# A new order for all steps of a delta-rule and MLP kernel, with forty instead of 26 filler products in its head

## The chip, the core and the metric

The kernel runs on one core of a Trainium2 chip. A core has five engines that run side by side, each through its own sequence of instructions: TensorE (PE, with its weight loads as PEld), VectorE (DVE), ScalarE (ACT), GpSimd (POOL) and SyncE (SP, which only issues transfers here). They wait for each other and for transfers on semaphores. The metric is the device time of one execution in microseconds (us); the median of several runs is compared.

## What is computed

The reference has two blocks. The first is a delta rule for 4 batches, 8 heads, 768 positions and head size 48: 32 independent states of 48 x 48, updated position by position.

```
k_n = k / (norm(k) + 1e-6)
for t in range(768):
    y[t]  = q[t] @ state
    v_old = state^T k_n[t]
    state = state + beta[t] * outer(k_n[t], v[t] - v_old)
```

Its output, laid side by side over the heads, is x with 768 positions of 384 features per batch. The second block is `x + relu(layernorm(x) * g @ w_ch1) @ w_ch2`, with w_ch1 of 384 x 1536 and w_ch2 of 1536 x 384. All numbers are 32-bit floats; the weights arrive as pairs of 32-bit words and are converted on the chip.

## The kernel before

**Chunks.** The 768 positions are cut into 12 chunks of 64. For each chunk TensorE forms the products of the keys with one another ("gram", L606 for chunks 0 to 4, L674 in a joint form later) and of keys with queries (L637, or jointly in L674). The triangular system of a chunk is inverted row by row on VectorE: for chunk 0 alone in a short form of 15 pairs of operations (L752 and L759, the near inverse), completed by two groups of small products on TensorE ("near products", L806: first xn x kt, then, after ScalarE's L809, xt x xn) and by a predicated copy on VectorE (L813); for two later chunks at once in 31 pairs (L843 and L850, the big inverse).

**The recurrence** runs chunk by chunk (`recur`): products with the state (L880), three solves (L902) with a copy on ScalarE (L908) or a subtraction on VectorE (L906) between them, the output y (L913), the state's update (L923), the layer normalization (L956 to L968) and the turned, scaled copy `xnt`. For chunk 0 there is no state yet, so it begins with the solves.

**The MLP** of a chunk follows its recurrence. For chunks 0 to 2 its first layer is done in plain products (L1178), for later chunks by fifteen block products with sums around them (L1094, with VectorE's L1107 and POOL's L1077). The second layer is plain for chunk 0 (L1200) and done by seven block products later (L1275, with POOL's L1261 and L1300). The weights are fetched in 12 pieces of 768 KB from ScalarE's queue and converted by ScalarE (L514, L522), VectorE (L519) and POOL (L532).

**The head.** Until the first MLP has its input, TensorE has little to do. Fillers are put there: 26 products of the identity with a broadcast column, 256 columns wide (`zeros`, L1358; each runs as two passes, so the profile counts 52), and three wider ones (`fill`, L544). They write half of a PSUM bank that nobody reads. The function `emit` lets other steps depend on them in no way (`or d.name == "warm"`), so they can stand anywhere in TensorE's sequence before that bank's half is wanted; nothing waits for them except what stands behind them on TensorE.

**The order.** The program first lists some 2,780 steps with what they read and write, without issuing anything. Then `line.emit(ORDER)` issues them in the order that the tuple `ORDER` names, by their numbers in the list. `in_this_order` ties each engine's instructions, and the transfers issued by SP and ScalarE, to that order. So `ORDER` sets the sequence of every engine and of both queues; between engines only data dependencies count. A transfer on these two queues also waits until the transfer eight places before it has landed, as eight semaphores are used in turn.

```
def emit(self, order):
    done = set()
    for n in order:
        s = self.steps[n]
        assert all(d.n in done or d.name == "warm" for d in s.deps), (n, s.key)
        done.add(n)
        s.fn()
```

Of the kernel before, what the change touches and what calls it, by code (L numbers as in the profile page):

```python
# [57 lines left out]
def pool(n):  # L58
# [5 lines left out]
WARM = 26  # L64
ORDER = (
    6, 7, 23, 5, 0, 59, 40, 60, 15, 8, 21, 4, 10, 20, 27, 16, 17, 219, 31, 26, 22, 69, 75, 29, 46, 35, 88, 89, 90, 67, 28, 25, 76, 92, 91, 93, 12, 94,
    1, 18, 2, 13, 126, 127, 19, 128, 129, 95, 3, 130, 30, 24, 131, 132, 133, 135, 9, 125, 134, 78, 65, 79, 61, 62, 81, 32, 385, 84, 34, 37, 42, 33,
    99, 101, 100, 50, 102, 41, 56, 86, 103, 104, 80, 47, 51, 48, 36, 64, 74, 38, 39, 82, 71, 96, 109, 107, 98, 66, 58, 97, 70, 110, 106, 108, 105, 53,
    322, 52, 44, 323, 202, 204, 190, 111, 114, 116, 115, 192, 117, 113, 72, 77, 87, 118, 119, 112, 121, 120, 179, 54, 68, 180, 43, 45, 321, 324, 169,
    136, 137, 138, 139, 140, 141, 142, 143, 144, 145, 146, 147, 148, 149, 150, 151, 152, 153, 154, 11, 155, 156, 170, 157, 158, 159, 160, 161, 162,  # L70
    203, 163, 164, 165, 171, 172, 166, 167, 191, 220, 205, 193, 173, 168, 174, 221, 175, 222, 122, 357, 181, 223, 14, 184, 352, 176, 196, 211, 177,
    206, 182, 124, 123, 194, 55, 224, 225, 226, 227, 228, 230, 231, 232, 233, 234, 235, 236, 237, 238, 239, 240, 241, 212, 242, 178, 243, 244, 245,
    246, 247, 229, 248, 249, 250, 251, 355, 252, 85, 293, 294, 295, 57, 296, 213, 326, 214, 215, 253, 183, 254, 255, 216, 256, 195, 257, 367, 297,
    188, 83, 561, 186, 258, 187, 259, 298, 299, 200, 301, 300, 260, 189, 382, 383, 63, 302, 303, 358, 304, 325, 319, 261, 198, 307, 305, 327, 262,
    306, 310, 263, 308, 328, 185, 197, 264, 311, 49, 265, 312, 73, 320, 266, 368, 360, 387, 388, 317, 267, 309, 703, 313, 390, 389, 268, 199, 269,
    329, 318, 343, 384, 315, 314, 316, 337, 567, 207, 333, 335, 330, 331, 270, 271, 272, 273, 570, 339, 340, 341, 342, 274, 275, 208, 276, 277, 359,
    391, 278, 392, 338, 566, 336, 279, 280, 427, 209, 332, 334, 425, 361, 426, 201, 394, 344, 372, 428, 429, 210, 362, 431, 353, 430, 432, 393, 217,
    218, 345, 435, 433, 281, 282, 283, 284, 285, 286, 287, 288, 289, 350, 351, 436, 290, 291, 292, 354, 386, 395, 439, 346, 434, 437, 370, 396, 705,
    568, 569, 563, 736, 560, 707, 564, 565, 841, 735, 369, 571, 348, 740, 716, 714, 701, 712, 840, 440, 349, 488, 438, 737, 739, 373, 715, 713, 397,
    711, 356, 717, 710, 441, 363, 442, 562, 398, 399, 464, 365, 445, 489, 400, 375, 487, 371, 465, 446, 490, 491, 449, 492, 493, 494, 495, 497, 496,  # L80
    498, 499, 500, 501, 502, 503, 374, 504, 364, 366, 401, 404, 405, 402, 406, 403, 407, 409, 410, 408, 411, 414, 376, 450, 451, 466, 467, 468, 469,
    718, 412, 479, 572, 452, 470, 471, 377, 443, 505, 453, 454, 506, 413, 507, 415, 416, 421, 508, 509, 510, 573, 417, 574, 444, 380, 472, 455, 456,
    423, 511, 512, 513, 514, 515, 378, 516, 517, 422, 518, 519, 447, 418, 379, 448, 480, 381, 419, 576, 733, 473, 474, 457, 520, 424, 475, 577, 420,
    575, 578, 521, 738, 743, 702, 522, 523, 747, 579, 998, 748, 704, 746, 745, 843, 997, 524, 525, 526, 527, 528, 529, 706, 485, 481, 996, 580, 742,
    749, 708, 709, 606, 476, 458, 459, 460, 461, 744, 750, 850, 581, 607, 848, 993, 582, 612, 851, 583, 613, 618, 608, 609, 530, 531, 532, 533, 584,
    482, 534, 719, 585, 610, 720, 619, 624, 614, 721, 625, 611, 616, 724, 615, 725, 620, 535, 536, 537, 639, 538, 539, 540, 541, 542, 483, 484, 543,
    544, 545, 546, 547, 548, 723, 549, 550, 551, 640, 641, 621, 722, 587, 590, 591, 552, 726, 730, 617, 595, 586, 588, 589, 622, 630, 642, 623, 347,
    596, 597, 727, 728, 893, 626, 729, 643, 627, 644, 890, 628, 645, 732, 631, 895, 636, 646, 633, 891, 838, 994, 845, 1174, 849, 839, 846, 852, 847,
    844, 734, 741, 478, 853, 477, 731, 632, 592, 486, 602, 1002, 634, 751, 462, 553, 635, 554, 1006, 656, 637, 555, 1177, 756, 657, 757, 1007, 752,
    658, 556, 593, 753, 659, 594, 1175, 629, 660, 754, 666, 638, 842, 755, 649, 650, 1003, 648, 557, 598, 1209, 758, 647, 558, 600, 1001, 896, 559,  # L90
    651, 1369, 763, 652, 599, 1176, 605, 653, 663, 764, 1000, 654, 759, 667, 760, 1005, 999, 668, 655, 761, 463, 669, 604, 762, 661, 1004, 674, 766,
    765, 670, 671, 854, 664, 767, 603, 601, 665, 675, 855, 676, 897, 677, 678, 662, 679, 672, 856, 673, 681, 858, 682, 683, 680, 684, 768, 898, 769,
    770, 771, 773, 772, 685, 899, 859, 775, 857, 776, 860, 777, 778, 779, 780, 861, 781, 782, 692, 783, 784, 686, 904, 785, 687, 786, 688, 862, 922,
    900, 1008, 892, 863, 787, 689, 788, 693, 864, 789, 694, 790, 695, 905, 696, 791, 865, 792, 867, 866, 1470, 1370, 910, 868, 1367, 870, 1184, 871,
    697, 1183, 911, 1009, 901, 698, 1365, 874, 793, 869, 923, 875, 1182, 794, 916, 699, 872, 1010, 1187, 1188, 902, 795, 1181, 796, 1366, 876, 906,
    1179, 797, 903, 880, 924, 1185, 873, 925, 798, 1172, 908, 907, 1368, 917, 799, 800, 1363, 1011, 801, 909, 1364, 877, 802, 995, 803, 931, 1013,
    1186, 912, 700, 878, 804, 1178, 805, 914, 1204, 806, 879, 1173, 807, 932, 881, 1014, 808, 882, 809, 1012, 1015, 810, 811, 913, 1016, 915, 812,
    928, 933, 1017, 894, 934, 935, 1180, 936, 918, 929, 937, 1189, 926, 1634, 1050, 948, 885, 949, 813, 920, 691, 938, 1378, 814, 1018, 690, 927, 921,
    815, 919, 884, 941, 930, 816, 1019, 1206, 942, 958, 940, 817, 886, 959, 1020, 939, 883, 818, 950, 1374, 819, 943, 1373, 820, 960, 961, 821, 1207,
    944, 822, 945, 1632, 823, 951, 889, 824, 1469, 962, 887, 956, 825, 963, 888, 1375, 946, 1058, 952, 1021, 1372, 953, 1054, 1022, 1663, 957, 947,  # L100
    964, 1379, 954, 965, 1190, 1468, 955, 1023, 1205, 973, 1055, 1194, 974, 1376, 1056, 975, 826, 1196, 1627, 976, 1057, 1191, 827, 977, 1192, 1061,
    1208, 1025, 966, 967, 1026, 828, 1062, 1029, 1195, 829, 830, 978, 831, 1063, 968, 979, 969, 1193, 774, 832, 970, 833, 971, 1030, 1031, 1065, 834,
    835, 836, 1197, 972, 1067, 837, 1045, 984, 1203, 985, 1198, 1202, 1059, 1081, 1199, 1035, 1210, 1200, 1066, 1068, 1201, 1024, 1027, 1070, 1060,
    1069, 1046, 1028, 1032, 1211, 1033, 1071, 1047, 1034, 1212, 986, 1064, 1036, 987, 1048, 1072, 1213, 1037, 1377, 1074, 1073, 1049, 988, 1075, 1214,
    980, 1371, 989, 981, 1215, 1079, 1474, 990, 991, 1076, 1629, 1052, 1216, 1824, 1077, 1038, 1083, 1080, 1053, 1633, 1082, 1040, 1095, 1084, 1051,
    992, 1086, 1217, 1085, 1041, 1092, 1395, 1039, 1087, 1821, 1380, 1218, 1088, 1078, 982, 1089, 1823, 1093, 1219, 1630, 1094, 1098, 1090, 1042,
    1101, 1044, 1096, 1220, 1043, 1251, 1099, 1110, 1249, 1925, 1221, 1100, 1102, 1111, 1252, 1112, 1640, 1113, 1107, 1636, 1114, 1115, 1246, 1641,
    1381, 1103, 983, 1104, 1642, 1117, 1222, 1387, 1662, 1386, 1105, 1097, 1120, 1822, 1116, 1108, 1121, 1382, 1471, 1091, 1122, 1385, 1127, 1106,
    1820, 1128, 1383, 1109, 1137, 1818, 1384, 1123, 1250, 1928, 1124, 1119, 1125, 1661, 1388, 1126, 1118, 1926, 1245, 1129, 1394, 1134, 1138, 1389,
    1390, 1130, 1247, 1145, 1391, 1135, 1146, 1396, 1131, 1248, 1147, 1148, 1149, 1397, 1132, 1398, 1399, 1150, 1133, 1253, 1151, 1400, 1224, 1401,  # L110
    1139, 1403, 1402, 1140, 1141, 1254, 1163, 1164, 1136, 1405, 1142, 1256, 1255, 1406, 1143, 1407, 1259, 1392, 1144, 1257, 1258, 1227, 1223, 1152,
# [108 lines left out]
def kernel(  # L220
# [1139 lines left out]
    for _ in range(3):  # L1360
        fill(1, 512, f_[3], FK[3])
    for _ in range(WARM):
        add("PE", 0.44, zeros, FK[0], [], np=2, arr=0.44, name="warm", after=["ident"])
# [110 lines left out]
```

## Time and profile before

| | |
|---|---|
| median of 3 runs | 508.15 us (505.75 to 508.51) |
| the profiled execution's own time | 508.88 us |
| its span, first to last instruction | 507.2 us |
| TensorE busy | 489.8 us, 97% |
| VectorE busy | 384.5 us, 76% |
| POOL busy | 246.1 us, 49% |
| ScalarE busy | 186.0 us, 37% |
| mean granted TensorE clock | 0.973 |

The page gives each engine's busy time, its share of the span and the number of instructions; then the span in 40 slices of 12.7 us, where a digit is the busy share in tenths and PEclk the clock granted to TensorE in tenths. A line of the timeline has the start in us, the length in us, the engine, the line of the program, the operation, the tiles written and read, the shape and, behind an x, how many instructions are merged in it; brackets tell the idle time before it and what ended it, where `issue` means that nothing in the profile explains the wait. A window line gives, for a stretch, each engine's busy us and count, the granted clock, the share of the transfer engines that was busy and GB/s. Products are pipelined, so their ends are modelled and neighbouring rows overlap a little.

### The profile page before, as it was taken

Reading aid. Unit: us, or ns where it says so; the run is one execution under the profiler, and the core shown is the slowest. Engines: PE = TensorE matmul, PEld = TensorE weight load, DVE = VectorE, ACT = ScalarE, POOL = GpSimd, SP = SyncE. Lnnn points to the kernel's source line nnn. Section 1 sums busy time; section 2 is a strip of 40 time slices with the busy share of each in tenths; the row PEclk is TensorE's granted clock in tenths of the full one; section 3 lists DMA queues with packets and bytes.
Section 4 is the critical chain, followed back from the end, with each engine's and each line's share of the span. In section 5 each row is a group of like instructions: output and inputs, shape, how many; then the busy total and the mean of one; then the engine's idle time right before and its main releaser. Section 6 shows DMA issues by size and latency. Waiting matters only on the chain.

```text
span 507.2 us, 21959 instructions
## 1 busy us (share of the span) xinstructions
PE 489.8 (97%) x9688; PEld 443.1 (87%) x9688; DVE 384.5 (76%) x854; ACT 186.0 (37%) x402; POOL 246.1 (49%) x377
## 2 busy tenths in 40 slices
PE   9958999999999999999999999999999999999996
PEld 6746876778888888999999989989999999999996
DVE  2869989988888688739899938998969799544241
ACT  3725964314612225352314523423332422233130
POOL 5221374123742448783383372492472672735563
PEclk9955899999999999999999999999999999999999
DMA  7987675715323654450562411622222300312011
GB/s 123 191 235 250 89 185 76 136 31 91 49 35 46 113 90 78 96 93 14 103 128 31 112 17 41 111 48 42 70 60 64 66 2 32 74 51 54 5 27 32
DMA packets 155855, 40.47 MB, mean 80 GB/s; under 512 B 149232, under 2 KB 152304, under 8 KB 155760
## 3 DMA queue, kind: packets, MB, share of 16 engines
q1 hardware_dynamic: 151760, 29.21, 31.9%
q10 hardware_dynamic: 3712, 9.83, 6.0%
q8 instruction: 76, 1.25, 1.0%
q14 instruction: 19, 0.16, 0.1%
q0 software_dynamic: 288, 0.03, 0.1%
HBM read 30.79 MB, written 8.26 MB: 77 GB/s over the span
## 4 chain that ended last, share of the span: by engine, by line
PE 73%; DMA 6%; POOL 6%; SPq 6%; DVE 4%; issue 3%; ACT 1%; POOLq 0%; DVEq 0%; ACTq 0%
PE f L1275 21%; PE f L1094 20%; PE f L1178 7%; SPq L373 6%; PE two L902 5%; POOL h_all L1261 3%; PE f L1200 3%; PE f L1358 3%; PE two L674 2%; PE two L880 2%; PE by L880 2%; DMA xnt<-xld 2%; PE by L913 1%; PE two L923 1%; POOL kt L1077 1%
## 5 line engine op out<-in xcount | busy, mean ns | idle before, releaser
L1261 POOL TENSOR_TENSOR h_all<-h_all 128x256 f32<-128x256 f32 x99 | 75.2, 768 | 27.0 <-ACT h_all L1187 18.1
L1275 PE MATMUL f<-w_sb,h_all 128*128 128x192 f32 x396 | 82.3, 333 | 0.0
L843 DVE TENSOR_TENSOR tmp<-xb,gb 128x31 f32<-128x31 f32 (+15 forms) x186 | 75.5, 406 | 4.5
L1107 DVE TENSOR_TENSOR h_all<-f,h_all 128x512 f32<-128x512 f32 x90 | 60.7, 685 | 21.8 <-PE f L1094 18.3
L1275 PE MATMUL f<-words,h_all 128*128 128x192 f32 x396 | 76.2, 330 | 0.3 <-POOL h_all L1261 0.2
L850 DVE TENSOR_TENSOR xb<-xb,tmp 128x31 f32<-128x31 f32 (+15 forms) x186 | 72.7, 391 | 3.8
L1275 PEld LDWEIGHTS f<-w_sb,h_all 128*128 128x128 f32 x396 | 64.8, 190 | 2.4 <-issue 0.6
L1275 PEld LDWEIGHTS f<-words,h_all 128*128 128x128 f32 x396 | 65.1, 190 | 2.0 <-POOL h_all L1261 0.9
L1300 POOL TENSOR_TENSOR words<-h_all 128x128 f32<-128x128 f32 x66 | 30.5, 481 | 65.6 <-ACT h_all L1110 43.7
L1178 PE MATMUL f<-xnt,w_sb 128*128 128x256 f32 x216 | 51.5, 385 | 0.6 <-issue 0.6
L1094 PE MATMUL f<-kt,w_sb 128*128 128x128 f32 x360 | 46.3, 276 | 1.1 <-DVE knrms L835 1.1
L1178 PEld LDWEIGHTS f<-xnt,w_sb 128*128 128x128 f32 x216 | 39.9, 190 | 7.0 <-issue 1.2
L1110 ACT ACTIVATE h_all<-h_all 128x512 f32<-128x512 f32 x54 | 32.6, 626 | 35.4 <-DVE h_all L1107 35.3
L1094 PEld LDWEIGHTS f<-kt,w_sb 128*128 128x128 f32 x360 | 43.3, 192 | 1.8 <-POOL kt L1077 1.3
L1102 ACT COPY h_all<-f 128x512 f32<-128x512 f32 x36 | 21.1, 586 | 62.3 <-PE f L1094 46.5
L908 ACT COPY u<-two 128x768 f32<-128x768 f32 x24 | 19.1, 798 | 57.3 <-PE two L902 41.9
L1293 POOL TENSOR_TENSOR o<-o,words 128x192 f32<-128x192 f32 x22 | 13.2, 609 | 51.8 <-DVE words L1293 51.8
L1094 PE MATMUL f<-xnt,w_sb 128*128 128x128 f32 x288 | 34.7, 277 | 0.0
L1094 PEld LDWEIGHTS f<-xnt,w_sb 128*128 128x128 f32 x288 | 33.4, 192 | 0.2
L1293 DVE TENSOR_TENSOR o<-f,x 128x192 f32<-128x192 f32 x33 | 11.3, 346 | 22.8 <-PE f L1275 16.9
L1275 PE MATMUL f<-w_sb,words 128*128 128x192 f32 x132 | 28.3, 332 | 0.0
L1187 ACT ACTIVATE h_all<-f 128x256 f32<-128x256 f32 x36 | 13.2, 384 | 38.0 <-PE f L1178 37.4
(198 smaller groups left out, 880.3 us busy)
## 6 DMA issues: line engine op xcount, KB each, us to landing
words<-in_moe_w_ch_dram ACTq DMA_DIRECT2D x8, 768.0 KB, 6.5
v<-in_v_dram SPq DMA_DIRECT2D x24, 192.0 KB, 3.9
kr<-in_k_dram SPq DMA_DIRECT2D x46, 96.0 KB, 3.3
out_dram<-o SPq DMA_DIRECT2D x46, 96.0 KB, 2.5
xld<-xlt SPq DMA_DIRECT2D x9, 384.0 KB, 2.6
xnt<-xld SPq DMA_DIRECT2D x36, 96.0 KB, 2.9
tb<-in_q_dram SPq DMA_DIRECT2D x40, 64.0 KB, 3.1
tb<-in_k_dram SPq DMA_DIRECT2D x32, 64.0 KB, 3.1
```

What stands on the lines that cost most here:

```text
L373: add(eng, cost, lambda: QUEUE[eng].dma_start(out=out_, in_=in_), r, w, bulk=n * ns / 16e3, pk=ns, **kw)
L843: lambda j=j, n=n, w=w, t=t: nc.vector.tensor_tensor(out=t, in0=xb[:, 0:n, j : j + 1].to_broadcast([128, n, w]), in1=gb[:, j : j + 1, j + ...
L850: "DVE", dve(n * w), lambda t=t, rest=rest: nc.vector.tensor_tensor(out=rest, in0=rest, in1=t, op=ALU.subtract),
L902: nc.tensor.matmul(*args(e, e ^ hp, 2 * j + hp))
L1094: nc.tensor.matmul(wide(p[:, 128 * n : 128 * n + 128]), w[:, 128 * n : 128 * n + 128], r, start=start and n == 0, stop=True, skip_group_ch ...
L1107: add("DVE", dve(512), lambda: nc.vector.tensor_tensor(out=to[0], in0=in0, in1=in1, op=op), [*pk, *y[1]], to[1])
L1110: add("ACT", act(512), lambda: nc.scalar.activation(to[0], to[0], ACTF.Relu), [], to[1])
L1178: nc.tensor.matmul(p[:, 0:TOK], w1_sb[:, t, f * 128 : (f + 1) * 128], xnt[:, t], start=(t == 0), stop=(t == KC - 1))
L1261: add(eng, cost, lambda: e.tensor_tensor(out=out_, in0=x, in1=y, op=op), r, w, port=2 if eng == "Pool" else 1)
L1275: lambda f=f, t=start and f == 0: nc.tensor.matmul(p[:, 0:D2], lhs(f), rhs[:, f], start=t, stop=(f == F2 - 1), skip_group_check=True),
L1293: lambda: e.tensor_tensor(out=out_, in0=a, in1=b_, op=ALU.add), r, w,
L1300: lambda f=f + i: e.tensor_tensor(out=s3[f], in0=one(0, 0)[0](f), in1=one(1, 0)[0](f), op=ALU.subtract),
```

## The change

`WARM`, the number of two-pass fillers in the list, goes from 26 to 40, so that the numbers of all later steps rise by 14; and `ORDER` is stated anew with 2,794 entries. The steps themselves, their tiles and their dependencies are the same. The new order is another sequence on every engine: of VectorE's 854 steps 525 can be lined up with their old sequence, of ScalarE's 416 some 210, of POOL's 373 some 179, and of the 321 on SP 76. On TensorE, 28 fillers (22 before) stand ahead of the first near product and 12 (4 before) behind it; the two halves of chunk 0's queries, which stood ahead of the first near product, stand between the two near products; the transposes of chunk 0's queries move behind chunk 2's gram; gram 3 stands between the last two groups of chunk 0's transposes (L1000). On VectorE, the query mask of chunk 0 (L653) moves from ahead of the big inverse to behind its tenth operation. On ScalarE's queue, the first weight piece is issued right behind the loads of chunk 0's keys.

```diff
 PASS = 0.015
 PLAN = None
-WARM = 26
+WARM = 40
 ORDER = (
...
 )
```

The lines inside `ORDER` are numbers alone and all of them differ.

## The prediction

> **What bounds the kernel now.** I read the page first: the busy table and the slices, then the queues.
>
> ```profile
> span 507.2 us, 21959 instructions
> ...
> PE 489.8 (97%) x9688; PEld 443.1 (87%) x9688; DVE 384.5 (76%) x854; ACT 186.0 (37%) x402; POOL 246.1 (49%) x377
> ...
> PEclk9955899999999999999999999999999999999999
> ...
> q8 instruction: 76, 1.25, 1.0%
> ```
>
> TensorE is busy throughout except in the head (25 to 56 us) and the last slice, and it runs at half clock in slices 3 to 5. From the first product of the first MLP (L1178, 59.73 us) to the end it is full: adding, for every TensorE step, the shortest time in which a step of its kind repeats (L1275 pair 0.325, L1094 step 0.891, L1178 step 1.295, L902 step 0.812 us) gives 424 of the 447 us between 55 and 503. Some 5 us of the rest are waits; most of the remainder are 0.09 us losses where a step of full products is followed by one of small products. Neither work nor shapes change there. So the head, and the question whether the new order holds TensorE as full, decide.
>
> Next the timeline of TensorE in the head (start, length, engine, line, tiles, count, idle before it):
>
> ```profile
> 24.02 0.45 PE L637 MATMUL two<-kq 48*64 48x64 f32 x12
> 27.80 0.91 PE L637 MATMUL two<-kq 48*64 48x64 f32 x20 [3.33 <-issue]
> 28.63 1.22 PE L1358 MATMUL f<-ident 128*128 128x256 f32 x2
> 29.78 1.13 PE L637 MATMUL two<-kq 48*64 48x64 f32 x32
> 30.85 1.27 PE L806 MATMUL f<-xn,kt 32*32 32x32 f32 x74
> 34.82 0.96 PE L806 MATMUL f<-xn,kt 32*32 32x32 f32 x54 [2.70 <-issue]
> 36.49 1.27 PE L806 MATMUL f<-xt,xn 32*32 32x32 f32 x74 [0.71 <-ACT xn L809]
> 38.27 0.96 PE L806 MATMUL f<-xt,xn 32*32 32x32 f32 x54 [0.51 <-issue]
> 39.16 1.22 PE L1358 MATMUL f<-ident 128*128 128x256 f32 x2
> 40.32 1.50 PE L902 MATMUL two<-v,xt 32*32 32x48 f32 x64
> ```
>
> Three gaps wait for nothing in the program. Between them stand 20+2+32+74 = 128 products, then 54+74 = 128. With a weight load each that is 256 instructions, and 2 x 9688 instructions over the 76 packets of the instruction queue are 255: TensorE runs out of instructions at the packets' edges. Counted through, edges lie at instruction 193 + 256k. From crossing one edge to being able to cross the next took 22.69 to 27.80, to 34.81, to 38.27, to 43.59: 5.1, 7.0, 3.5 and 5.3 us, while weights come in. The Trainium skill ("Runtime: NRT & Kernel Launch", Instruction fetch mechanics) gives the same 256 and calls a block's cost "mostly hidden"; the trace has 3.33 us in the open.
>
> Last the windows (us, then busy and count of PE, PEld, DVE, ACT, POOL, clock, DMA):
>
> ```profile
> 27.00:27.50 0.50, 0.00 (x0) 0.00 (x0) 0.00 (x0) 0.38 (x2) 0.50 (x1) 0.68 1.12 419
> 54.00:56.00 2.00, 1.70 (x32) 1.23 (x27) 1.97 (x6) 1.34 (x3) 0.00 (x0) 0.88 0.82 118
> 63.40:76.00 12.60, 12.04 (x313) 9.95 (x305) 10.43 (x19) 7.59 (x17) 9.27 (x8) 1.00 0.76 185
> 76.00:88.80 12.80, 12.80 (x306) 8.80 (x310) 11.71 (x27) 6.40 (x13) 5.83 (x5) 1.00 0.58 76
> 88.80:101.40 12.60, 12.60 (x165) 9.04 (x154) 12.01 (x29) 4.04 (x10) 1.91 (x1) 1.00 0.72 137
> 101.40:127.00 25.60, 25.60 (x590) 20.83 (x589) 22.18 (x47) 7.76 (x20) 7.92 (x9) 1.00 0.36 60
> 127.00:152.00 25.00, 24.84 (x546) 22.19 (x545) 21.32 (x41) 10.46 (x30) 15.14 (x20) 1.00 0.29 43
> ```
>
> The clock halves at 27.2 (0.68 is 0.18 us whole and 0.32 us half), 2.7 us into the first gap, and is whole again at 54.5 (0.88): 27.3 us. And VectorE has little room up to 152 us.
>
> **The change part by part.** Instructions other than the 14 fillers stay; each engine's sequence is new. Lines are those of before.
>
> Fillers (L1358). One costs 0.85 us at the cold start (four halves from 4.71 to 6.41), 0.47 at full clock (14 halves in 3.31), 1.16 in the half-clock stretch (39.16 to 40.32). Before the first near product (L806, xn x kt) stand 28 instead of 22, behind it 12 instead of 4. Of the six, one is cold, ahead of the first transposes; TensorE has no idle there, so its cover is only a late load of k, and I charge 0.85. The other five cost 2.25. The two query halves (L637, 1.1 us) move behind the near product, so TensorE reaches that at 25.4 (24.02 plus the rest without the gap) + 3.1 - 0.9 = 27.6.
>
> VectorE in front of it. The near inverse carries more strangers: masks, memsets and a 768-wide shift (0.56), some 2.3 against 1.5 us that nothing hides. With the 0.85 the near product's input is ready at 24.97 + 0.85 + 0.8 = 26.6, so TensorE's 27.6 counts. The first weight load is issued right behind the first four k loads instead of at 14.61; bounds 0 (under the fillers) to 1.8 us (a later weight load's halves, 24.15 to 29.91 on the chain, against the 3.3 us median of a k load, shared); I take 0, as the third filler covers 0.85. POOL makes the identity behind more of its own small work, near 3.7 instead of 1.4, under the wide fillers (to 4.9).
>
> To chunk 0's first solve (L902, now 40.32). The edge that opened at 27.80 now falls five instructions into the near product, the next right behind it, the next in the middle of the second one, and one 11 instructions before that solve's end. Crossing 23.6 instead of 22.69 (three more fillers, two transposes fewer ahead) gives 27.0 to 28.7 with 3.5 to 5.1 us; the further two at 3.5 to 7.0 and 3.5 end the second product between 36.5 and 40.2 (now 39.23). VectorE: the big inverse of chunks 1 and 2 no longer waits for the query mask (idle 4.26 at 30.98), so it starts at 30.9 instead of 34.58; but the mask (1.23) and four more of its operations stand ahead of the predicated copy, whose turn is 37.9. The solve starts at 38.9 to 41.3. I take 40.1: -0.2.
>
> Solve to y0's end (40.32 to 50.76 now). Six fillers instead of one. At half clock: one filler and the transposes against a 0.92 us wait, +0.8; three (3.5) against the 1.27 us that VectorE's subtraction takes, +2.2; two (2.3) against 1.1, +1.2; one gap of 0.48 goes: +3.7. At full clock fillers hide, the three solves shrink from 1.5 to 0.81 and y0 from 1.96 to 0.97: -3.1. If the clock returns behind the three fillers: +0.8. Half clock comes from the gap behind the near product (29.9 to 32 or 35.7, longer than the 2.7 us that sufficed). I take 2.2, between the half-clock ends, as no row decides between them.
>
> Y0 to the first L1178 (8.97 us now). Four fewer inverse operations (0.41 each) stand in the normalization, which begins 0.5 later: -1.1. Gram 3 moves ahead of the last transposes and one filler behind them: -0.95 at full, +0.7 at half clock; together -0.4 in the half-clock case. Head: -0.2 + 2.2 - 0.4 = +1.6.
>
> VectorE after the head. In the new order 342.5 of its 384.5 us lie behind the first L1178, in the old 337.7: 4.8 more remain. I summed, from there, VectorE's durations up to each of its steps and TensorE's up to that step's first user. The smallest lead was 8.1 (60 us on) and 10.7 (86 us on); it is 3.9 and 5.7. The windows show VectorE idle for 9.7 us by 84 us on, so 1.0 was left. Were all that idle forced, TensorE would wait 4.0; if idle gives way, as an engine running late finds inputs ready, 0. I take 2.0.
>
> Elsewhere: changes from full to small products 83 instead of 79, 0.4. ScalarE, POOL and the SP queue keep their instructions; in the same sum ScalarE's and POOL's leads stay within 2 us of the old ones and pass 15 us by 40 us on, which covers them; without it a wait would cost what before's own did, 0.2 to 1.2. A load on SP or ScalarE waits until the eighth before it has landed, so chunk 1's last k load now waits for the early weight load; it is wanted only by the transposes at 15 us (13.53 before), behind seven fillers, and costs nothing unless it lands later. The tail holds the same chain (POOL sums, then the output); 0, -1 to +1.
>
> Sum: 1.6 + 2.0 + 0.4 = +4.0 on the profiled 508.88 (span 507.2, 1.7 around it): 512.9; that execution stands 0.7 over the median of 508.15, so **512.2** as a median.
>
> **Rivals.**
> The clock stays whole (the other side). If the gap behind the near product stays under 2.7 us, as with 3.5 us per edge, the clock does not fall, and the head is -0.2 - 3.1 - 1.1 - 0.95 = -5.4. With 2.0 + 0.4: 505.2; with no VectorE wait 503.2. For it: the fillers close the idle up to 27.6. Against: the edges took 5.1 and 7.0 in this stretch.
>
> The clock falls but returns early. TensorE is full from the solve on. If 3.4 us of that suffice, the three fillers run half at each clock (the middle of +0.8 and -3.1, -1.2) and the rest at full: -0.2 - 1.2 - 1.1 - 0.95 = -3.4, total 507.1. Against: the full stretch from 47.65 to 51 did not bring it back. The Trainium skill ("TensorE: Matmul & The Clock Gate", Part 1) has one busy window of about 3.4 us restore the clock; by it this rival wins. The trace has 27.3 us.
>
> VectorE falls behind. The whole 4.0, and again where chunk 6's gram and chunk 3's queries (L674, L637, 134 to 141 us) had 0.2 to 0.5 us of room behind their masks, 2 more; with +3.1 in the head: 508.15 + 3.1 + 6 + 0.4 = 517.7.
>
> Nothing moves: the earlier start of the big inverse pays for the fillers, VectorE's idle gives way: 508.15 + 0.4 = 508.6.
>
> **How the numbers follow.** Forecast 0.37 (own range 510 to 515), whole clock 0.18, early return 0.12, VectorE behind 0.18, nothing 0.15. Range 503.5 to 519: it leaves out the far ends of both. The measurement tells some 0.5% (2.5 us) from no change. Faster (under 505.6): most of whole clock, a little of early return, 0.21. Same: the rest of these two, nothing, and the forecast's lower edge, 0.26. Slower: 0.53.
>
> **What would show it.** PEclk: halves near 31 and not at 27, whole again before 56. TensorE gaps put down to issue behind the first L806 group and in the middle of the second. The first L902 at 39 to 41, the first L1178 at 60 to 63. Waits of small products on VectorE between 80 and 150 us. Wrong if PEclk has no half at all, if the first L1178 starts before 57, or if body waits exceed 10 us anywhere after 150.

## The result and the profile after

The changed kernel took 509.94 us as a median of 13 runs (506.85 to 515.24), the kernel before 507.71 (13 runs, 505.44 to 510.89) in the same comparison. The ratio is 1.0057, with a 95% interval of 1.0036 to 1.0077: slower by some 2.9 us by the ratio, by 2.2 between the medians. The profiled execution took 509.79 us (span 508.1), the one of before 508.88 (span 507.2). So the two profiles differ by 0.9 us only; before's profile stands 1.2 above the median of its 13 runs, after's 0.15 below its own.

In the changed kernel every line number behind `ORDER` is one higher than before (L806 is now L807).

Busy times and the granted clock, from the page of the changed kernel:

```profile
span 508.1 us, 22020 instructions
...
PE 490.5 (97%) x9716; PEld 443.4 (87%) x9716; DVE 387.7 (76%) x854; ACT 186.8 (37%) x402; POOL 248.3 (49%) x377
...
PEclk9987999999999999999999999999999999999999
```

The 28 more TensorE products (and as many weight loads) are the 14 fillers. The clock digits sink only in slices 3 and 4 (25 to 51 us), to 8 and 7: TensorE was at half clock for 10.2 us instead of 27.3.

The timeline of TensorE in the head, same columns as in the prediction:

```profile
4.71 2.51 PE L1359 MATMUL f<-ident 128*128 128x256 f32 x6
8.45 1.06 PE L556 MATMUL by<-ident,kr 128*128 128x128 f32 x8 [1.23 <-DMA kr<-in_k_dram]
...
30.25 0.70 PE L1359 MATMUL f<-ident 128*128 128x256 f32 x2 [0.86 <-issue]
30.88 1.27 PE L807 MATMUL f<-xn,kt 32*32 32x32 f32 x126
37.27 0.31 PE L807 MATMUL f<-xn,kt 32*32 32x32 f32 x2 [5.12 <-issue]
37.51 1.99 PE L638 MATMUL two<-kq 48*64 48x64 f32 x64
39.43 1.07 PE L807 MATMUL f<-xt,xn 32*32 32x32 f32 x62
40.73 1.16 PE L807 MATMUL f<-xt,xn 32*32 32x32 f32 x66 [0.23 <-issue]
41.82 1.11 PE L556 MATMUL f<-ident,tb 128*128 128x128 f32 x4
42.73 1.84 PE L1359 MATMUL f<-ident 128*128 128x256 f32 x4
44.50 0.78 PE L903 MATMUL two<-v,xt 32*32 32x48 f32 x52
45.64 0.36 PE L903 MATMUL two<-v,xt 32*32 32x48 f32 x12 [0.35 <-issue]
...
49.26 0.88 PE L903 MATMUL two<-v,xt 32*32 32x48 f32 x64
...
51.64 0.65 PE L914 MATMUL by<-u,pt 64*64 64x48 f32 x32
...
55.02 0.67 PE L924 MATMUL two<-u,kr 64*64 64x48 f32 x30 [1.39 <-issue]
...
61.45 2.75 PE L1179 MATMUL f<-xnt,w_sb 128*128 128x256 f32 x12
```

The edges of the instruction blocks (instruction 193 + 256k, as counted in the prediction) can be set side by side. Between one pair of gaps stand again 126 + 2 = 128 products (the filler's two and 126 of the near product), between the next 2 + 64 + 62 = 128.

| crossing of the edge at instruction | before | after | difference |
|---|---|---|---|
| 705 | 22.69 | 25.28 | 2.59 |
| 961 | 27.80 | 30.25 | 2.45 |
| 1217 | 34.82 | 37.27 | 2.45 |
| 1473 | 38.27 | 40.73 | 2.46 |
| 1729 | 43.59 | 45.64 | 2.05 |

The blocks arrive at the same pace in both kernels: 5.1 and 5.0 us, 7.0 and 7.0, 3.5 and 3.5. What stands at the edges is other work, but the whole chain is late by what edge 705 was late, and most of that comes from the very start: the first transposes, at 6.41 before, stand at 8.45. Their row says why: 1.23 us of waiting for a load of k, the rest being the third filler ahead of them.

That these waits are waits for instructions can be read from the trace directly, as it holds the packets of the instruction queue (q8, 16 KB each) with their times. In before, packets landed at 26.29, 33.37, 36.86 and 42.19, and TensorE crossed an edge 1.4 to 1.5 us behind each (27.80, 34.82, 38.27, 43.59); in after they landed at 28.69, 35.66, 39.30 and 44.16, with the crossings 1.4 to 1.6 us behind (30.25, 37.27, 40.73, 45.64). A packet itself took 0.9 to 1.6 us. What differs is when it started: 4.4 us behind the crossing at 30.25, but 1.1 behind the one at 37.27. What held its start back is not shown.

From edge 1473 on two paths lead to chunk 0's first solve. VectorE's is this:

```profile
35.44 0.29 DVE L851 TENSOR_TENSOR xb<-xb,tmp 128x135 f32<-128x135 f32 x1
39.57 1.22 DVE L654 TENSOR_TENSOR pt<-two,pmask 128x1024 f32<-128x1024 f32 x1 [3.83 <-PE two L638]
...
43.38 0.72 DVE L814 COPY_PREDICATED xt<-mask,f 128x512 f32<-128x512 int32 x1
```

The query mask waits 3.83 us for the query halves, which stand behind the late block; the predicated copy, with eight operations between the mask and it, starts 1.5 us after the second near product has ended (41.89), where before it followed at once, and is done at 44.10.

TensorE's path is in the rows at 41.82 and 42.73: four transposes and two fillers stand between the second near product and the solve, where before there was one filler. At half clock they keep TensorE without a gap until 44.50, 2.6 us behind the near product's end, where before it was 1.1 (39.23 to 40.32). This path ended last. So the first solve comes at 44.50 instead of 40.32, 4.2 us late: 2.7 because the second near product ends later, 1.5 because of the transposes and the second filler. In the variants of this head described below, too, the solve always follows its fillers without a gap; in after_weights_late the copy was done at 43.27 and the solve still began at 44.37, when the fillers ended.

Then most of that comes back. The windows of 3.41 us around it (columns as in the prediction's windows):

```profile
34.13:37.54 3.41, 0.27 (x6) 0.20 (x6) 1.50 (x6) 0.00 (x0) 0.00 (x0) 0.50 0.72 228
37.54:40.96 3.42, 3.19 (x143) 2.94 (x146) 1.39 (x2) 3.32 (x7) 0.00 (x0) 0.50 0.71 228
40.96:44.37 3.41, 3.41 (x74) 2.72 (x65) 3.24 (x10) 2.05 (x4) 0.83 (x1) 0.50 0.82 287
44.37:47.78 3.41, 3.06 (x136) 2.33 (x135) 3.27 (x9) 1.70 (x3) 0.99 (x2) 1.00 0.50 86
```

The clock is whole again from 44.37, just ahead of the solves. The third one takes 0.88 us instead of 1.50, and from the first solve to y0's end pass 7.8 us (44.50 to 52.29) instead of 10.44, as the rows of before show beside those above:

```profile
46.21 1.50 PE L902 MATMUL two<-v,xt 32*32 32x48 f32 x64 [0.22 <-DVE v L906]
...
49.69 1.07 PE L913 MATMUL by<-u,pt 64*64 64x48 f32 x32
```

The first L1179 starts at 61.45, 1.7 late. From there to the end the new order takes 446.6 us, the old 447.4.

### The profile page after: what moved, and what is told of

Same layout as the page of the kernel before. It is cut to its first block, busy times and chain, and to the rows that moved or that the text cites. A ratio compares the mean times of both kernels' runs of the same rounds, so it can differ in the third digit from the quotient of the medians.

```text
span 508.1 us, 22020 instructions
## 1 busy us (share of the span) xinstructions
PE 490.5 (97%) x9716; PEld 443.4 (87%) x9716; DVE 387.7 (76%) x854; ACT 186.8 (37%) x402; POOL 248.3 (49%) x377
## 4 chain that ended last, share of the span: by engine, by line
PE 51%; SPq 2%; DMA 2%; POOL 1%; issue 1%; DVE 1%; ACT 0%; POOLq 0%; DVEq 0%
PE f L1095 21%; PE f L1276 21%; PE two L903 3%; SPq L374 2%; PE two L881 1%; PE by L914 1%; PE two L675 1%; PE by L881 1%; PE two L924 1%; POOL h_all L1262 1%; DMA out_dram<-o 1%; DMA xld<-xlt 1%; DMA kr<-in_k_dram 1%; DVE h_all L1108 0%; POOL o L1294 0%
## 5 line engine op out<-in xcount | busy, mean ns | idle before, releaser
L1276 PE MATMUL f<-w_sb,h_all 128*128 128x192 f32 x396 | 80.2, 330 | 0.0
L851 DVE TENSOR_TENSOR xb<-xb,tmp 128x31 f32<-128x31 f32 (+15 forms) x186 | 75.4, 405 | 3.9
L1301 POOL TENSOR_TENSOR words<-h_all 128x128 f32<-128x128 f32 x66 | 31.3, 492 | 58.3 <-ACT h_all L1111 41.3
L1179 PE MATMUL f<-xnt,w_sb 128*128 128x256 f32 x216 | 50.6, 383 | 0.4 <-issue 0.4
L1179 PEld LDWEIGHTS f<-xnt,w_sb 128*128 128x128 f32 x216 | 40.1, 190 | 6.4 <-issue 1.0
L909 ACT COPY u<-two 128x768 f32<-128x768 f32 x24 | 19.1, 798 | 58.1 <-PE two L903 47.5
L533 POOL TENSOR_TENSOR w_sb<-words 128x768 uint32<-128x768 uint32 (+1 forms) x9 | 12.4, 1383 | 38.3 <-DVE words L520 24.4
L1294 POOL TENSOR_TENSOR o<-o,words 128x192 f32<-128x192 f32 x22 | 13.7, 630 | 35.5 <-DVE words L1294 35.5
```

The lines of the kernel that those rows point to most:

```text
L851: "DVE", dve(n * w), lambda t=t, rest=rest: nc.vector.tensor_tensor(out=rest, in0=rest, in1=t, op=ALU.subtract),
L909: add("ACT", act(768), lambda: nc.scalar.copy(u_j, p_2), TWO, uk, after=() if c else ["nought", *SMALL])
L1179: nc.tensor.matmul(p[:, 0:TOK], w1_sb[:, t, f * 128 : (f + 1) * 128], xnt[:, t], start=(t == 0), stop=(t == KC - 1))
L1276: lambda f=f, t=start and f == 0: nc.tensor.matmul(p[:, 0:D2], lhs(f), rhs[:, f], start=t, stop=(f == F2 - 1), skip_group_check=True),
L1294: lambda: e.tensor_tensor(out=out_, in0=a, in1=b_, op=ALU.add), r, w,
L1301: lambda f=f + i: e.tensor_tensor(out=s3[f], in0=one(0, 0)[0](f), in1=one(1, 0)[0](f), op=ALU.subtract),
```

## The experiments

All ratios are to the kernel before, run on the same chip in the same comparison, each from 6 to 13 runs of the changed kernel and 11 to 17 of before. "Head" is the start of the first product of the MLP (L1178, or L1179 where lines are shifted) in the profile, "rest" what is left of the span from there.

| kernel | head | rest | ratio (95% interval) |
|---|---|---|---|
| before | 59.73 | 447.4 | 1 |
| after | 61.45 | 446.6 | 1.0057 (1.0036 to 1.0077) |
| head_old_rest_new | 57.46 | 450.5 | 1.0107 (1.0060 to 1.0155) |
| head_new_rest_old | 66.99 | 449.5 | 1.0179 (1.0137 to 1.0222) |
| new_fillers26 | 66.17 | 446.1 | 1.0075 (1.0045 to 1.0105) |
| old_fillers40 | 60.82 | 451.6 | 1.0189 (1.0150 to 1.0228) |
| before_narrow | 61.40 | 454.1 | 1.0212 (1.0172 to 1.0251) |
| after_weights_late | 66.88 | 447.2 | 1.0100 (1.0069 to 1.0132) |
| after_w58_late | 66.75 | 444.7 | 1.0162 (1.0137 to 1.0188) |
| before_queries_late | 60.57 | 446.9 | 1.0057 (1.0037 to 1.0076) |
| after_filler_behind | 64.05 | 447.2 | 1.0106 (1.0070 to 1.0141) |
| after_near_whole | 64.03 | 446.2 | 1.0151 (1.0113 to 1.0190) |
| after_wide | 65.86 | 445.1 | 1.0128 (1.0085 to 1.0170) |
| before_wide | 58.76 | 445.2 | 0.9989 (0.9967 to 1.0011) |

Head and rest are read from one execution each, and such an execution can stand some 3 to 4 us from its kernel's median: new_fillers26's stands 3.8 above, head_new_rest_old's and after_weights_late's 3.2 above, old_fillers40's 2.9 below. One and the same sequence of the head took 59.73 and 57.46 us (before and head_old_rest_new) and 61.45 and 66.99 (after and head_new_rest_old). So heads that lie less than some 5 us apart do not by themselves show what an edit did.

**Two halves.** The entries of `ORDER` up to the first L1178 were taken from one kernel, the remaining ones from the other.

```diff
# head_old_rest_new; head_new_rest_old is its mirror
 ORDER = (
...  entries of before up to the first L1178
-    the other entries in the sequence of before
+    the other entries in the sequence of after
 )
```

> Steps up to chunk 0's first product of the MLP (L1178) in the order of before, with 26 fillers; all steps behind it in the order of after. In the two profiles the changed kernel loses 1.7 us up to that product and gains 0.8 behind it; between the medians it loses some 2.5. Theory H, the head carries the loss: this kernel is no slower than before, ratio 0.997 to 1.001, first L1178 at 59 to 60.5 us. Theory V, the new order behind the head (VectorE's thinner lead) carries it: ratio 1.004 to 1.008 although the first L1178 stands where it stood.

> The other half: steps up to the first L1178 in the order of after, with 40 fillers; all behind it in the order of before. Theory H: ratio 1.004 to 1.009, half clock for about 10 us from 34, first L1178 at 61 to 62 us. Theory V: ratio 0.998 to 1.002. If this and its counterpart both stand above 1.003, the two orders do not mix and the test tells nothing.

Both ratios stand above 1.003, the case named beforehand in which the orders do not mix. The profile of head_old_rest_new shows where the mixture pays:

```profile
57.46 2.86 PE L1178 MATMUL f<-xnt,w_sb 128*128 128x256 f32 x12
64.16 5.81 PE L1178 MATMUL f<-xnt,w_sb 128*128 128x256 f32 x18 [3.84 <-ACT h_all L1187]
```

The next products wait 3.84 us; the row of that group's weight load (PEld, at 64.13) names POOL's conversion of w_sb (L532, 4.21 us), and the conversion's own row a wait for ScalarE's (L522). The weights come late, as the new order has their conversions elsewhere. Two things can still be read. With the new sequence behind a head that is 4 us shorter than after's, the trace shows no wait of 0.2 us or more of TensorE's products on VectorE behind the head. And in head_new_rest_old the head's sequence is that of after, but the profiled execution stayed at half clock for 20.5 us instead of 10.2, and its first L1179 stands at 66.99 instead of 61.45: with one sequence, the head differs by 5.5 us between two executions.

**The fillers alone, both ways.** new_fillers26 takes 14 fillers out of the new order; old_fillers40 puts 14 into the old one, everything else in place.

```diff
# new_fillers26
-WARM = 40
+WARM = 26
 ORDER = (
...  as after, less six fillers ahead of the near product and eight behind it
 )
# old_fillers40
-WARM = 26
+WARM = 40
 ORDER = (
...  as before, six more ahead of the near product and eight more behind it
 )
```

> The order of after in every step that computes, but with 26 fillers at about the places where before has them (22 ahead of the near product, 4 behind it). Theory C, the extra fillers cost TensorE time ahead of the near product: its start (30.88 in after) moves 2 to 3 us ahead, ratio 0.997 to 1.001. Theory K, the extra fillers behind the near product are what brought the clock back after 10.2 us: without them half clock stays some 27 us, the stretch from the first L902 to y0's end is 10 us again instead of 7.7, ratio 1.005 to 1.012.

> The order of before in every step that computes, with 14 more fillers at about the places where after has them (28 ahead of the near product, 12 behind). Theory C: each filler ahead costs its 0.47 (0.85 when cold) and those in half clock 1.16, together 3 to 5 us at most, ratio 1.003 to 1.008, half clock still some 27 us. Theory K: the clock comes back after 10 us, which is worth 2 to 4 us and pays for them, ratio 0.996 to 1.001.

Theory C fails in both. Without the fillers the near product starts at 30.05 instead of 30.88, not 2 to 3 us ahead, its edges come at 31.89, 39.46 and 45.11, half clock lasts 27.3 us (and 6.8 more from 10 us on, behind a wait of 2.37 us for k), and the first L1178 is 4.7 us later than in after, in an execution 3.8 us above its kernel's median. That is theory K's outcome, yet K fails in the other kernel. There the clock does come back sooner, with two spells of half clock of 6.8 us in the head instead of one of 27.3, but the head is 1.1 us longer all the same, and the rest loses 4.2 us; its largest wait alone is 4.22:

```profile
67.37 1.15 PE L881 MATMUL two<-s_all,kq 48*64 48x48 f32 x64
68.45 1.37 PE L607 MATMUL f<-kq 48*32 48x64 f32 x117
74.04 0.44 PE L607 MATMUL f<-kq 48*32 48x64 f32 x11 [4.22 <-issue]
```

That is an edge, too: the last 11 products of one group and 117 of the next, all small, use up a block in 1.7 us, and the block behind it is not there: its packet landed at 72.65, 1.4 us ahead of the crossing. In before the edges fall elsewhere, and the nearest wait at one is 0.56 us. Fourteen fillers are 56 instructions; they shift every later edge by that much.

**Edges without work.** To test that, edges were shifted in the old order with its 26 fillers, first one way, later the other.

```diff
# before_narrow: edges 56 instructions earlier in the work
-    for _ in range(3):
-        fill(1, 512, f_[3], FK[3])
+    fill(8, 64, f_[3], FK[3])
+    fill(8, 64, f_[3], FK[3])
+    fill(1, 512, f_[3], FK[3])
# before_wide: 8 pairs of neighbouring fillers become one of 512 columns, edges 32 later
-    for _ in range(WARM):
-        add("PE", 0.44, zeros, FK[0], [], np=2, arr=0.44, name="warm", after=["ident"])
+    for n in range(WARM):
+        cols = 512 if n in WIDE else 256
+        add("PE", 0.44, lambda cols=cols: zeros(cols), FK[0], [], np=2, arr=0.44, name="warm", after=["ident"])
```

> The order of before with its 26 fillers, but the first two wide zero products (512 columns each, at 1.13 us) are cut into 16 of 64 columns: the same columns, 28 more product-and-load pairs, so all edges of TensorE's instruction blocks lie 56 instructions further back in the work, as in the kernel with 14 more fillers, with no work added. Theory E, where the edges fall decides: the gap of about 4 us at the edge near 74 us shows up as it did in the order of before with 40 fillers, the ratio is 1.006 to 1.014. Theory C, the fillers' own time cost what that kernel lost: ratio 0.998 to 1.002, no body gap over 1.5 us.

> The order of before with the same filler time, 8 pairs of fillers made into one of 512 columns each: all edges behind 25 us lie 32 instructions later in the work. If the order is as sensitive to that as it was to 56 the other way (3.99 us at 74 us and two half-clock spells in the body): any body gap shows at an edge that falls into small products, and the ratio lies 0.003 or more from 1 on either side. If the earlier harm was special to that one shift: ratio 0.997 to 1.003, the edge near 73 us costs 0 to 0.6.

In before_narrow:

```profile
1.13 7.09 PE L544 MATMUL f<-u 128*128 128x64 f32 x32 [1.13 <-DVE u L390]
...
74.58 0.44 PE L606 MATMUL f<-kq 48*32 48x64 f32 x11 [3.99 <-issue]
```

The wait at 74 us is there again, at the same eleven products, with no filler added: theory E. The ratio went further than the 1.006 to 1.014 expected. One part is the edit itself: 32 passes of 64 columns take 7.09 us where four of 512 took 3.78, so the first transposes come 3.4 late and the head ends 1.7 late. The other is the clock: two spells of half clock in the rest, 6.8 us from 72.2 and 3.4 from 157.5, behind the waits of 3.99 and 0.86 us. So the rest is 6.7 us longer. The shift the other way did no harm: the edge near 73 us costs nothing, the head is 1.0 shorter, the ratio 0.9989 cannot be told from 1. It falls under the second reading, that the harm belongs to particular shifts. It is the only kernel here that is level with before; its median of 505.54 us (before 506.10) makes it the better choice against after.

**What delays the chain.** Two loads were moved in the new order: the first weight piece (step 58), issued right behind the first k loads, and the piece that is in flight while the block behind 32.15 us is wanted (step 366).

```diff
# after_w58_late
-    90, 22, 81, 58, 26, 31, 24,
+    90, 22, 81, 26, 31, 24,
...
-    28, 108, 30,
+    28, 108, 58, 30,
# after_weights_late
-    126, 198, 366, 138, 218,
+    126, 198, 138, 218,
...
-    187, 194, 191, 338, 337,
+    187, 194, 191, 366, 338, 337,
```

> The order of after, only the first weight load stands behind chunk 0's first gram instead of right behind the first k loads. If that load takes its bandwidth from the k loads (first transposes at 8.45 instead of 6.41 in before, of which the third filler accounts for 0.6), they start at 7.0 to 7.4 and their wait of 1.23 us on the load of k is gone; if this then carries through, the first L1179 is 0.8 to 1.5 us earlier and the ratio to before 1.002 to 1.004. If the chain of instruction blocks sets the pace from 25 us on, the 1.2 us are lost there and the ratio stays 1.004 to 1.008.

> The order of after, only the weight load that starts at 29.90 us (second half of chunk 0's second weights) stands behind the second near product. In after two weight loads run from 28.99 and 29.90 to 36 us, and the instruction block wanted at 32.15 us comes at 37.27. Theory F, the weights hold that block up: the wait of 5.12 us shrinks to 2 to 4, the first L903 solve moves from 44.5 to 41.5 to 43.5, half clock 10 us or less, ratio to before 0.998 to 1.004. Theory G, the block takes its 7 us anyway: wait 4.8 to 5.4, ratio 1.004 to 1.008.

In after_w58_late:

```profile
6.35 1.04 PE L556 MATMUL by<-ident,kr 128*128 128x128 f32 x8
...
18.73 1.94 PE L556 MATMUL f<-ident,kr 128*128 128x128 f32 x8 [5.10 <-DMA kr<-in_k_dram]
```

The wait on the first k is gone and the first transposes stand at 6.35, even with the third filler. So the early weight load is what made them late. But SyncE's queue now waits 8.5 us for the weight load to land (issued at 9.59), so that its next two loads of k are issued at 15.74 instead of 9.01; chunk 1's transposes wait 5.10 us for k, and everything behind is 5 us later than in after: edges at 35.40, 42.43 and 45.88, the wait in the near product again exactly 5.12. Neither expected outcome came true for the total, as neither had the next loads of k wait for this one.

In after_weights_late the wait of 5.12 shrinks to 3.47 and the block takes 5.4 us instead of 7.0: with one of the two weight loads away it comes earlier, theory F; its packet started 2.7 us behind the crossing instead of 4.4. One pair does not settle it, as head_old_rest_new, with no load moved, has a block of 5.4 us where before has 7.0. Nothing is gained: the two edges behind it now cost 1.06 and 1.57 us, where they cost 0.23 and 0.35, and the first solve stands at 44.37 (after: 44.50). Half clock lasts 20.5 us in two spells, and the ratio of 1.0100 lies above both ranges.

**What stands at the edges.** Three kernels change which work the late block interrupts: the query halves behind the second near product in the old order; one filler moved behind the near product in the new one, so that its last two products are no longer cut off; and that with the query halves and the query mask put back as well.

```diff
# before_queries_late: steps 179, 180 (L637) behind 177, 181 (L653) behind 178
-    120, 179, 54, 68, 180, 43,
+    120, 54, 68, 43,
...
-    211, 177, 206,
+    211, 177, 179, 180, 206,
...
-    122, 357, 181, 223,
+    122, 357, 223,
...
-    242, 178, 243,
+    242, 178, 181, 243,
# after_filler_behind: a filler from ahead of step 189 (first near product) to behind it
-    238, 239, 189, 204, 240,
+    238, 239, 189, 89, 204, 240,
# after_near_whole: that filler, 193 and 194 (L638) behind 191 (second near product), 195 behind 192
-    187, 194, 191, 338,
+    187, 191, 89, 193, 194, 338,
```

> The order of before with its 26 fillers, only the two query halves (L637) stand behind the second near product instead of ahead of the first, and the query mask behind the predicated copy. If the near inverse's chain up to the first solve is what TensorE's missing instruction blocks hold up, taking 64 products out of that chain lets the second near product end at 34 to 37 instead of 39.2 us and the first solve start at 37 to 39 instead of 40.3: ratio 0.993 to 0.999. If the blocks' pace or VectorE's inverse sets it all the same: 0.999 to 1.003.

> The order of after, only one filler (four instructions) moved from ahead of the near product to right behind it, so that all 128 products of the near product (L807) lie inside one instruction block, where in after its last two lie behind the edge. Theory N, the near product's late end is what the wait of 5.12 us costs: ScalarE's copy of it (L810, 37.62 us in after) starts at 32 to 33, the first L903 solve at 41 to 43, ratio to before 0.999 to 1.003. Theory P, the pace of the blocks sets the time whatever stands at their edges: the wait moves to the filler or the query halves, which end at 39 to 40 as before, the first solve starts at 43.8 to 44.8, ratio 1.003 to 1.007.

> As the kernel with one filler moved, and the two query halves (L638) behind the second near product, the query mask behind the predicated copy. Theory N: the second near product starts at 37.3 instead of 39.4 us and the first solve at 41 to 43, ratio 0.998 to 1.002. Theory P: three block edges stand before the solve's end either way (30, 37 and 41 us, and the fourth at 45 to 46 inside or just behind the first solve), so the third product (L903 u x goff) starts at 46 to 47.5 as in after, ratio 1.003 to 1.007.

before_queries_late shows best that the place of the work does not help:

```profile
31.29 1.82 PE L806 MATMUL f<-xt,xn 32*32 32x32 f32 x118 [0.97 <-issue]
...
38.03 1.77 PE L637 MATMUL two<-kq 48*64 48x64 f32 x54 [4.31 <-issue]
...
41.18 1.50 PE L902 MATMUL two<-v,xt 32*32 32x48 f32 x64 [0.23 <-issue]
```

The second near product ends at 33.1 instead of 39.2, better than expected. But the edge at instruction 1473 is crossed at 38.03 (before: 38.27), now by the query products, and the first solve starts at 41.18, later than the 40.32 of before. The expected 0.993 to 0.999 was a miss: 1.0057.

In after_filler_behind all 128 near products run in one piece and the wait moves to the filler behind them (5.46 us, at 38.54), as theory P has it; ScalarE's copy comes at 34.74 instead of 37.62. Yet the solve starts at 47.88, later than P's range, because this execution also waited 1.99 us for the first k, so that edge 961 stands at 31.79 (the row names VectorE, but a packet landed 1.5 us ahead of it), and waited 1.51 us at edge 1473 (after: 0.23). In after_near_whole the second near product meets the edge (37.84, a wait of 5.73), the filler the next (42.67, 2.89), and the first solve stands at 47.69: the predicated copy is done at 40.56, but the queries, transposes and two fillers stand ahead of the solve on TensorE and come last. P's place for the third product (46 to 47.5) is exceeded too, at 49.54. Theory N falls in both; how much of the ratios above after's belongs to the edit and how much to these executions' later k is open.

**Edges and fillers in the new order.** Same filler time, 56 instructions less:

```diff
-WARM = 40
+WARM = 26
+WIDE = {0, 4, 5, 6, 7, 8, 9, 10, 11, 12, 16, 17, 19, 21}
...  fillers of 512 columns as in before_wide
```

> The order of after with the same filler time, but 14 pairs of neighbouring fillers (256 columns each) made into one of 512, so 56 instructions less ahead of the later edges. With 26 narrow fillers instead, the first product of the MLP came 4.7 us later than in after. Theory E, the edges' place did that: it comes at 64 to 67 us here too, ratio to before 1.005 to 1.012. Theory K, TensorE's missing filler time did it (it was at half clock from 10 to 17 and from 34 to 61 us): with the time back it comes at 60 to 62.5, half clock 10 to 20 us, ratio 0.998 to 1.006.

The first L1179 stands at 65.86, as theory E expected, and the ratio is just above its range. But the head shows that it is not the edges' times alone: the first transposes start at 6.51, the edges stand at 29.25, 36.00 and 40.82, the first of them 1.0 ahead of after's, and the first solve at 44.35 is as early as after's. What differs is the clock, still half in these windows:

```profile
43.28:46.69 3.41, 3.41 (x70) 2.22 (x69) 2.95 (x7) 0.72 (x2) 1.57 (x2) 0.50 0.00 0
46.69:50.11 3.42, 3.42 (x69) 2.16 (x68) 0.80 (x1) 2.54 (x5) 1.06 (x2) 0.50 0.51 157
50.11:53.52 3.41, 3.41 (x69) 2.10 (x67) 2.97 (x8) 0.00 (x0) 0.00 (x0) 0.50 0.21 80
53.52:56.93 3.41, 3.41 (x58) 1.91 (x62) 0.89 (x2) 1.91 (x3) 1.12 (x1) 0.50 0.02 5
```

TensorE is busy without a break, and the clock stays half until 57. It is not so in every execution: a run's half-clock time is twice what its mean granted clock is short of 1, times its span, and three runs of this kernel at a mean clock of 0.986 to 0.987 (13 to 14 us) took 509.3 to 511.0 us, two at 0.972 and 0.973 (28 us) 516.3 and 516.0. So executions of one kernel stand some 5 us apart with the time at half clock.

## Why the prediction was right, and where it was not

The forecast was 512.2 us, in a range of 503.5 to 519, with slower as the likeliest; 509.94 came, slower. The total was nearer than its terms, and that is luck: in the head two errors of more than 4 us cancel, and the +2.0 for VectorE did not come.

**The head, +1.6: measured +1.7, from terms that missed in both directions.** The first solve was put at 40.1 (-0.2) and came at 44.50 (+4.2). From it to y0's end +2.2 was charged and -2.7 measured. From y0's end to the first L1178 -0.4 was charged, +0.2 measured; in it lies a wait of 1.39 us at one more edge (L924, 55.02), which was not counted and which before does not have.

*The first solve.* The step that failed is "Crossing 23.6 instead of 22.69", with the early weight load taken as costing 0 out of 0 to 1.8. The crossing came at 25.28. In the changed kernel the k loads made TensorE wait 1.23 us, and in six of the seven profiles with that load at its early place 1.2 to 2.4; with it moved the wait was gone. The idea that "the third filler covers 0.85" was wrong: the wait came on top of the filler. The pace of the blocks was rightly read (3.5 to 5.1, 3.5 to 7.0 and 3.5 us, measured 5.0, 7.0 and 3.5, each before's own), but it was counted from a start that was too early, and not from its slow end. The place of one edge was misread as well: it lay not five instructions into the near product but four ahead of it, so that the next one cut off the product's last two; after_filler_behind, which has them in one piece, is no faster. The rest is the step from the second product's end to the solve. The upper bound of 41.3 adds to 40.2 what the single filler of before takes; the four transposes and the second filler that the new order puts there were left out, and they cost 1.5 us more. The step "whose turn is 37.9" failed too, but did not decide: the mask was counted ahead of the predicated copy, not the mask's own wait of 3.83 us for the query halves, which the change had put behind the late block. The copy's turn came at 43.38, and it was done 0.4 us before TensorE was free.

*The clock.* The condition was right: the gap in the near product halves the clock. That it then stays half through the solves, taken "as no row decides", was wrong in the profile: it was whole from 44.37. That is the rival "the clock falls but returns early". It charged -1.2, with the clock back at the three fillers behind the second solve. The clock was back ahead of the first solve, and the -2.7 measured is nearer to the -3.1 that the prediction gives for this stretch at full clock. The rival's total of 507.1 failed on the first solve's +4.2. So the forecast and this rival each had one half.

**VectorE's lead, +2.0: it did not come.** Behind the first L1179 the new order takes 446.6 us against 447.4, and 444.7 to 447.2 in the six variants that keep its sequence throughout. The wait of small products on VectorE looked for between 80 and 150 us is not in the trace (none of 0.2 us or more). The own lower bound, that idle gives way when an engine runs late, was the right end. With 1.7 us more of head VectorE also has 1.7 more of lead, but head_old_rest_new, 2.3 us shorter than before in the head, shows no such wait either.

**83 instead of 79 changes of shape, +0.4.** Not to be seen apart: it lies inside the -0.8 of the rest.

**The sum.** Forecast +4.0, the profiles show +0.9, the medians +2.2. The difference between the last two is not found in any row. Before's profile stands 1.2 above its median, so that much may be this execution. Its clock fits that: by the mean granted clock it was at half clock for 27 us, where most other executions of before had 24 (0.976), while after's profile, with 10 us, has the least of the 13 executions of after (10 to 19). How much time that is stays open. One reading of before was also too high: of the "some 5 us" of waits between 55 and 503 us the trace shows 3.3 as idle time of TensorE.

**The other rivals.** The clock whole: no, it fell at 34.1. VectorE behind: no. Nothing moves: its time of 508.6 is nearer to the result than the forecast, but its reason, the earlier big inverse paying for the fillers, is not what happened. Of the signs named beforehand, the first L1178 at 60 to 63, the clock back before 56 and the gaps put down to issue in both near products came true; the fall came at 34, not near 31, and the first solve at 39 to 41 did not.

**What the loss is.** That it lies in the head rests on the rest being no longer in any of the seven kernels with the new order throughout, while their heads are 61.45 to 66.9 us against 59.73, one execution each. That the early weight load delays the first transposes is shown by moving it, with the first loads of k issued at the same times. That the 14 fillers' own time is the loss is refuted: with 14 taken out the kernel is no faster (1.0075 against 1.0057), and put into the old order they cost 1.9%, more than the 3 to 5 us that theory C gives for their time. That their 56 instructions can matter more than their time is shown at the edge near 74 us, which waits 3.99 us in before_narrow without an added filler; part of that kernel's loss is its longer start. Which part of the new order costs the 2.9 us is not isolated: no piece of it that was moved or mixed gave them back. That a faster arrival of the one late block would have saved it is not shown: the wait shrank and the head did not.

## What to carry to other kernels

Where TensorE runs thousands of small products, its instruction blocks are a resource with a pace of their own; count the edges through the trace, set the instruction queue's packets beside them, and price an added instruction also by where it puts every later edge. An order that was settled with one number of fillers is settled for those edges, so fillers, loads and order have to be changed and measured together. A transfer that is moved has to be followed to whichever load shares its time, and to whichever load waits for it to land, at its new place as well as at its old one. And when a unit seems to wait for one engine, look at what its own queue still had to do: here the solve's copy came late, but TensorE's own fillers came later.

## What the runs showed of the hardware that was not expected

A shift of 56 instructions, without other work behind the head, gave a wait of 3.99 us at an edge inside 128 small products (before_narrow), and a spell of half clock of 6.8 us with it. At the edges in the head at which it had waited, TensorE went on 1.2 to 1.8 us after an instruction packet had landed, in all fourteen profiles. A block took 3.5 to 7.6 us from crossing to crossing, of which the packet itself took 0.9 to 1.7; most of the rest lay ahead of its start. It was shorter with one weight load moved away (5.4 instead of 7.0), but also once without that, so the weights' part is open. The Trainium skill ("Runtime: NRT & Kernel Launch", Instruction fetch mechanics) calls the crossing "mostly hidden"; in the rest of before that holds, with 0.73 us of such waits in all, and in the head of after it does not, 5.12 at one edge.

All half-clock spells of the fourteen profiles last a multiple of 3.41 us, within the 0.1 us at which the trace was read: 3.4, 6.8, 10.2, 13.7, 20.5, 23.9 and 27.3. The Trainium skill ("TensorE: Matmul & The Clock Gate", Part 1) states such a window (3413 ns, running freely), and the trace agrees. It also states that one busy window restores the clock, which the runs do not bear out as the profile counts busy: before had the window from 47.66 to 51.07 full and stayed at half, after_wide had three in a row. Those windows held 42 to 55% products of 32 or 64 rows, the rest transposes and fillers of 128 rows; in after the window that ended the spell held 75% of the latter. But the share of rows does not decide either: the window that ended the spell in before (51.07 to 54.49) held the same 45% as the one ahead of it, and in after_wide one with 55% ended it behind three with 58%. What ends a spell stays open.
